# MLP weight tiles placed at rotating byte offsets, and the second layer's input moved by 224 bytes

## The chip, the cores and the metric

The kernel runs on one core of one Trainium2 chip. The metric is device time in microseconds (us) for one execution of the whole program; smaller is better. The core's engines run side by side and meet at semaphores: TensorE (PE, matmuls; its weight loads are shown as PEld), VectorE (DVE), ScalarE (ACT), GpSimd (POOL) and SyncE (SP, which issues the DMAs). Operands of a matmul lie in SBUF, 128 partitions with one address space in each; its result goes to PSUM.

## The reference

```python
x = A_u                                          # (1, 2048, 448)
mod = (silu(c) @ w_mod).reshape(c.shape[0], 6, 1, -1)
sa, ca, ga, sb, cb, gb = (mod[:, k] for k in range(6))
h = layernorm(x) * (1 + ca) + sa
x = x + ga * S4D(h)                              # a convolution over the 2048 tokens, by FFT in the reference
h = layernorm(x) * (1 + cb) + sb
# token-mixing MLP
h = layernorm(h)                                 # (1, 2048, 448)
u = gelu(einsum("bsd,sf->bdf", h, w1) + b1)      # w1: 2048 x 1792
y = einsum("bdf,fs->bds", u, w2) + b2            # w2: 1792 x 2048
x = x + gb * y.transpose(0, 2, 1)
```

All arrays are float32. The part that matters here is the MLP at the end: two products with weight matrices of 2048 x 1792 and 1792 x 2048, each against 448 channels.

## The kernel before

The first 57% of the program computes the modulation, the S4D convolution (with transforms written as matmuls) and the sum with `x`. The MLP follows, and there TensorE has hardly a gap.

**The MLP's split.** Each product is made with three matmuls in `float32r`, a form of float32 that TensorE takes in one pass. A weight tile `w` (128 partitions x 896 elements) is split into a high part `whi` (ScalarE, line 207) and a low part `wlo` = `w` - `whi` (VectorE, line 216). The other side is split in the same way: the normed input into `h3h` and `h3l`, the gelu's output into `uh` and `ul`. Then come high x high, high x low and low x high: lines 1373 to 1375 in the first layer (the function `mlp1`), lines 1442 to 1444 in the second. The weights are the stationary operand, 128 x 128 at a time (the weight load, PEld); the other side streams past them, 128 x 448 (the moving operand). That makes 672 matmuls in each layer, 1344 in all.

**The weight stream.** `WeightStream` numbers 64 weight tiles, n = 0 to 31 for the first layer and 32 to 63 for the second. `load` issues the DMA of a tile into one of 3 buffers of `w`; `begin` makes the high part, `rest` the low part and the next load. `whi` and `wlo` have `WAHEAD` = 4 buffers each, so the split runs up to four tiles ahead of the matmuls and then waits for a buffer.

**Where things lie.** The pools hand out SBUF addresses; the weight pool `mw` stands at the right end of SBUF, and the pools `mx` (the sums `xt`) and `mr` (layer norm's scratch) lie to its left. The pools `mk` (`h3h`, `h3l`) and `mu` (`uh`, `ul`) are filled from the left. A slice of 128 weight columns is 512 bytes, a row of a moving operand 1792 bytes, which is 7 x 256, a buffer of `whi` or `wlo` 3584 bytes, which is 14 x 256. So the address modulo 256 of a tile is that of all its slices and of all its buffers. In the program before, every slice of `whi` and `wlo` begins at 224 modulo 256, and every row of `h3h`, `h3l`, `uh` and `ul` at 32. For brevity this number is called the operand's place below.

The order of the work in the MLP is written out by hand on TensorE, ScalarE, VectorE and GpSimd (`manual_schedule`).

Of the kernel before, what the change touches and what calls it, by code (L numbers as in the profile page):

```python
# [11 lines left out]
F32 = mybir.dt.float32  # L12
F32R = mybir.dt.float32r
# [9 lines left out]
P = 128  # L23
# [13 lines left out]
WAHEAD = 4  # L37
# [117 lines left out]
def token_rows(a):  # L155

    return a.rearrange("(n g h r) d -> r g n h d", g=2, h=2, r=16)
# [8 lines left out]
class WeightStream:  # L166
# [4 lines left out]
    def __init__(self, tc, ctx, i):  # L171
        self.nc = tc.nc
        self.pool = ctx.enter_context(tc.tile_pool(name="mw", bufs=WAHEAD, side="right", reuse_waits="tile"))
        self.w1 = token_rows(i["B_w1"])
        self.w2 = i["B_w2"].rearrange("(k p) s -> p k s", p=P)
        self.raw, self.parts = {}, {}
        self.loaded = self.done = 0

# [20 lines left out]
    def begin(self, most):  # L199

        n = self.done
        if n >= min(most, 64):
            return None
        w = self.raw.pop(n)
        hi = self.pool.tile([P, 896], F32R, tag="whi", name="whi")
        lo = self.pool.tile([P, 896], F32R, tag="wlo", name="wlo")
        self.nc.scalar.copy(hi, w)  # L207
        self.parts[n] = hi, lo
        self.done += 1
        return w, hi, lo  # L210
# [11 lines left out]
def tile_adaln_s4d_mixer(ctx, tc, i, out):  # L222
# [21 lines left out]
    with ExitStack() as es:  # L244
# [827 lines left out]
        for s in range(tail):  # L1072
# [89 lines left out]
            if s == 16:  # L1162
                spec.close()
                up = early.enter_context(tc.tile_pool(name="up", bufs=3, reuse_waits="tile"))
# [190 lines left out]
    with ExitStack() as es:  # L1355
# [3 lines left out]
        up = es.enter_context(tc.tile_pool(name="mu", bufs=1))  # L1359
        pacc = es.enter_context(tc.tile_pool(name="pacc", bufs=7, space=PSUM))  # L1360
        h3h = kp.tile([P, 16, D], F32R, name="h3h")
        h3l = kp.tile([P, 16, D], F32R, name="h3l")
        uh = [up.tile([P, 7, D], F32R, name="uh0"), None]
        ul = [up.tile([P, 7, D], F32R, name="ul0"), None]

# [65 lines left out]
        for t in range(16):  # L1431
# [4 lines left out]
            for kh in range(2):  # L1436
                n = 32 + 2 * t + kh
                wst.ahead(n + WAHEAD, V)
                hi, lo = wst.parts.pop(n)
# [36 lines left out]
```

## Time and profile before

| | us |
|---|---|
| median of 3 runs | 690.65 (687.97 to 694.99) |
| the profiled execution | 685.43 |
| its span, first to last instruction | 683.7 |
| matmuls of the MLP, first to last start | 393.7 to 678.6 |
| TensorE busy in all | 612.7 (90%) |

The profiled execution took 1.7 us more than its span, and 5.2 us less than the median of the runs. A row that describes a group of instructions reads: line, engine, operation, out<-in by the program's names, shapes, count, then busy time in us and mean ns of one, then idle time before them with what ended it. A matmul's duration is from its start to its last result; the next one starts before that, so what a matmul costs in a stream is the distance from its start to the start of the next. PEclk is the granted share of TensorE's clock.

### The profile page before, as it was taken

What the parts mean: (1) busy time and instruction counts of PE and PEld (TensorE: products, weight loads), DVE (VectorE), ACT (ScalarE), POOL (GpSimd) and SP (SyncE); (2) the same over time, 40 slices, a digit from 0 to 9 for tenths busy, and PEclk for the clock granted to TensorE, in tenths of its full rate; (3) what the DMA queues carried; (4) which work ended last, traced back from release to release, by engine and by line L of the source; (5) the groups of instructions that cost most, each with busy time, mean ns of one, the idle gap of its engine ahead of it and who ended that gap; (6) DMA issues with size and microseconds to landing.
All of it is one profiled execution on the core that took longest, in us unless ns stands there. A gap on an engine that the chain in (4) does not pass through costs nothing. (4 is left out here: it accounts for less than half of the span.)

```text
span 683.7 us, 18263 instructions
## 1 busy us (share of the span) xinstructions
PE 612.7 (90%) x7180; PEld 456.0 (67%) x7180; DVE 452.6 (66%) x870; ACT 439.0 (64%) x880; POOL 268.1 (39%) x323
## 2 busy tenths in 40 slices
PE   0786778879989899989989899999999999999997
PEld 0443345535535556565657677779999999999996
DVE  7498799888779596895967587777422454433331
ACT  5967597988988999999945588877322322222220
POOL 6397457448458889789847100000000000000000
PEclk9989888999999999999999999999999999999999
DMA  7695563377896857344359799956674355555530
GB/s 176 199 201 111 181 200 120 128 269 223 251 310 190 234 116 216 97 133 136 97 140 315 237 256 255 239 128 199 160 221 135 95 142 168 165 161 170 167 119 28
DMA packets 105923, 121.14 MB, mean 177 GB/s; under 512 B 13098, under 2 KB 94286, under 8 KB 105710
## 3 DMA queue, kind: packets, MB, share of 16 engines
q1 hardware_dynamic: 104478, 113.92, 58.1%
q0 software_dynamic: 1360, 6.06, 4.1%
q8 instruction: 57, 0.93, 0.6%
q14 instruction: 28, 0.23, 0.1%
HBM read 84.59 MB, written 34.87 MB: 175 GB/s over the span
## 5 line engine op out<-in xcount | busy, mean ns | idle before, releaser
L207 ACT CAST whi<-w 128x896 fp32r<-128x896 f32 x64 | 59.8, 940 | 132.2 <-PE o L1443 84.5
L679 POOL TENSOR_TENSOR G<-mag,gs 128x512 f32<-128x512 f32 x56 | 71.8, 1281 | 66.1 <-ACT gs L675 65.9
L216 DVE TENSOR_TENSOR wlo<-w,whi 128x896 fp32r<-128x896 f32 x64 | 68.0, 1086 | 40.3 <-ACT whi L207 27.9
L1373 PE MATMUL acc<-h3h,whi 128*128 128x448 f32 x224 | 83.3, 372 | 1.6 <-ACT h3h L1278 1.6
L1374 PE MATMUL acc<-h3l,whi 128*128 128x448 f32 x224 | 82.1, 367 | 0.1
L1443 PE MATMUL o<-ul,whi 128*128 128x448 f32 x224 | 81.3, 363 | 0.0
L1375 PE MATMUL acc<-h3h,wlo 128*128 128x448 f32 x224 | 81.2, 362 | 0.0
L1442 PE MATMUL o<-uh,whi 128*128 128x448 f32 x224 | 81.2, 362 | 0.0
L1444 PE MATMUL o<-uh,wlo 128*128 128x448 f32 x224 | 80.6, 360 | 0.0
L710 PEld LDWEIGHTS kg<-E,G 128*32 128x32 f32 x3584 | 57.3, 116 | 34.9 <-issue 14.5
L627 PE MATMUL xg<-tab,lph 64*128 64x512 f32 x112 | 62.9, 563 | 12.4 <-DVE E L687 4.7
L710 PE MATMUL kg<-E,G 128*32 128x64 f32 x3584 | 67.1, 230 | 7.0 <-issue 3.3
L680 POOL TENSOR_TENSOR G<-mag,gs 128x512 f32<-128x512 f32 x56 | 71.8, 1282 | 0.0
L627 PE MATMUL xe<-tab,lph 64*128 64x512 f32 x112 | 63.5, 569 | 4.7 <-ACT gs L676 2.6
L1446 DVE SCALAR_TENSOR_TENSOR y<-o,b,mod 128x448 f32<-128x448 f32 x16 | 10.9, 684 | 80.2 <-PE o L1444 80.2
L656 POOL TENSOR_TENSOR m<-mag,w 128x512 f32<-128x512 f32 x56 | 58.9, 1052 | 4.4
L681 DVE TENSOR_TENSOR E<-m,xe 128x512 f32<-128x512 f32 x56 | 38.1, 681 | 23.2 <-ACT xe L674 19.8
L1373 PEld LDWEIGHTS acc<-h3h,whi 128*128 128x128 f32 x224 | 42.4, 189 | 14.6 <-ACT h L1283 5.6
L627 PE MATMUL xe<-tab,lex 64*128 64x512 f32 x56 | 30.9, 569 | 19.2 <-DMA lex<-wm 17.0
L1375 PEld LDWEIGHTS acc<-h3h,wlo 128*128 128x128 f32 x224 | 42.3, 189 | 3.0
L1442 PEld LDWEIGHTS o<-uh,whi 128*128 128x128 f32 x224 | 42.0, 188 | 3.4
L1374 PEld LDWEIGHTS acc<-h3l,whi 128*128 128x128 f32 x224 | 42.4, 190 | 2.7 <-DVE h3l L1281 0.5
(239 smaller groups left out, 1440.1 us busy)
## 6 DMA issues: line engine op xcount, KB each, us to landing
w<-in_B_w_dram SPq DMA_DIRECT2D x64, 224.0 KB
w<-in_B_w_dram SPq DMA_DIRECT2D x32, 448.0 KB
yu_d<-yt SPq DMA_DIRECT2D x16, 448.0 KB
yi<-yu_d SPq DMA_DIRECT2D x16, 448.0 KB
us_d<-uo SPq DMA_DIRECT2D x16, 448.0 KB
u<-us_d SPq DMA_DIRECT2D x32, 224.0 KB
v_d<-vt SPq DMA_DIRECT2D x32, 224.0 KB
vt<-v_d SPq DMA_DIRECT2D x14, 448.0 KB
```

The lines of the kernel that those rows point to most:

```text
L207: self.nc.scalar.copy(hi, w)
L216: eng.tensor_tensor(lo, w, hi.bitcast(F32), ALU.subtract)
L627: T.matmul(out[k], lhs[r], rhs[r], start=start, stop=stop)
L679: G.tensor_tensor(Gt[:, 1], mg_, v32(sg), ALU.mult)
L680: G.tensor_tensor(Gt[:, 0], mg_, v32(cg_), ALU.mult)
L710: T.matmul(kgs[g][32 * q : 32 * q + 32, m], Gt[:, c, d], E[:, c, d], start=h == 0 and c == 0 and m == 0, stop=h == 1 and c == 1, skip_grou ...
L1373: nc.tensor.matmul(acc[f], hi[:, fs], h3h[:, r], start=r == 0, stop=False)
L1374: nc.tensor.matmul(acc[f], hi[:, fs], h3l[:, r], start=False, stop=False)
L1375: nc.tensor.matmul(acc[f], lo[:, fs], h3h[:, r], start=False, stop=r == 15)
L1442: nc.tensor.matmul(o, hi[:, ks], uh[kh][:, k], start=kh == 0 and k == 0, stop=False)
L1443: nc.tensor.matmul(o, hi[:, ks], ul[kh][:, k], start=False, stop=False)
L1444: nc.tensor.matmul(o, lo[:, ks], uh[kh][:, k], start=False, stop=kh == 1 and k == 6)
```

## The change

Three tags of the weight pool are now asked for ahead of the others, so that they get their addresses in this order: `w` (3 x 3584 bytes), `whi` (4 buffers, now 920 elements = 3680 bytes), and a `gap` of 128 bytes; `wlo` (4 x 3680 bytes) follows. A buffer of 3680 bytes is 14 x 256 + 96, so each buffer's start is 96 further modulo 256 than the one before. Four of them and the gap make 58 x 256: a buffer of `wlo` has the same place as the buffer of `whi` of the same number. Within its buffer, the tile n begins at 8 x (n // 4 % 4) elements, so 0, 32, 64 or 96 bytes, for four tiles each. The pool `mu` gets 56 more elements, 224 bytes, ahead of `uh` and `ul`.

```diff
         self.w2 = i["B_w2"].rearrange("(k p) s -> p k s", p=P)
+        for t, m, b in (("w", 896, 3), ("whi", 920, WAHEAD), ("gap", 32, 1)):
+            self.pool.tile([P, m], F32R if t == "whi" else F32, tag=t, name=t, bufs=b)
         self.raw, self.parts = {}, {}
...
         w = self.raw.pop(n)
-        hi = self.pool.tile([P, 896], F32R, tag="whi", name="whi")
-        lo = self.pool.tile([P, 896], F32R, tag="wlo", name="wlo")
+        at = 8 * (n // 4 % 4)
+        hi, lo = (self.pool.tile([P, 920], F32R, tag=t, name=t)[:, at : at + 896] for t in ("whi", "wlo"))
         self.nc.scalar.copy(hi, w)
...
         h3l = kp.tile([P, 16, D], F32R, name="h3l")
+        up.tile([P, 56], F32, name="gap0")
         uh = [up.tile([P, 7, D], F32R, name="uh0"), None]
```

The addresses of the two built programs, modulo 256 (the buffers are taken in the order 0, 3, 2, 1):

| | before | after |
|---|---|---|
| `whi`, `wlo`, tiles n = 0 to 3 | 224 | 96, 128, 32, 192 |
| n = 4 to 7 | 224 | 128, 160, 64, 224 |
| n = 8 to 11 | 224 | 160, 192, 96, 0 |
| n = 12 to 15, and so on every 16 tiles | 224 | 192, 224, 128, 32 |
| `h3h`, `h3l` (moving, first layer) | 32 | 32 |
| `uh`, `ul` (moving, second layer) | 32 | 0 |
| `w` (landing of the weight DMAs) | 224 | 96 |

The pools `mx` and `mr` lie 896 bytes lower than before. The instructions of each engine, their order, the semaphores they wait for and their shapes are the same in both programs, row for row; only addresses differ.

## The prediction

> **What bounds the kernel now.** I read the page first: its chain of waits, then the groups of instructions, and then TensorE's stretch in the second layer.
>
> ```profile
> span 683.7 us, 18263 instructions
> PE 42%; ACT 1%; DVE 1%; issue 0%; ACTq 0%
> L1373 PE MATMUL acc<-h3h,whi 128*128 128x448 f32 x224 | 83.3, 372 | 1.6 <-ACT h3h L1278 1.6
> L1443 PE MATMUL o<-ul,whi 128*128 128x448 f32 x224 | 81.3, 363 | 0.0
> L1442 PE MATMUL o<-uh,whi 128*128 128x448 f32 x224 | 81.2, 362 | 0.0
> L1444 PE MATMUL o<-uh,wlo 128*128 128x448 f32 x224 | 80.6, 360 | 0.0
> ```
>
> The chain ends in TensorE for 42% of the span, and its lines are the MLP's matmuls. The right-hand column is the idle time in front of them: 0.0 in the second layer. Next, the stretch of that layer by busy time, and the tile `uh` with the first and last start of line 1442.
>
> ```profile
> core 0: us, PE busy (x) PEld busy (x) DVE busy (x) ACT busy (x) POOL busy (x), PEclk, DMA share, GB/s
> 544.00:678.50 134.50, 134.50 (x674) 126.06 (x674) 54.09 (x70) 29.85 (x33) 0.00 (x0) 1.00 0.50 141
> L1442 PE MATMUL o<-uh,whi x224: 362/362/363, 544.4 to 678.2; 128*128 128x448 f32 x112
> ```
>
> TensorE is busy for all of the 134.5 us, at a granted clock of 1.00, while VectorE is busy for 54 us and ScalarE for 30. Line 1442 comes once in three matmuls: 678.2 - 544.4 = 133.8 us over 223 steps is 600 ns for three, so 200 ns for one. The timeline of TensorE and of its weight loads shows the step itself (start in us, duration in us):
>
> ```profile
> 560.02 0.36 PE L1442 MATMUL o<-uh,whi 128*128 128x448 f32 x1
> 560.23 0.36 PE L1443 MATMUL o<-ul,whi 128*128 128x448 f32 x1
> 560.43 0.36 PE L1444 MATMUL o<-uh,wlo 128*128 128x448 f32 x1
> 560.62 0.36 PE L1442 MATMUL o<-uh,whi 128*128 128x448 f32 x1
> ...
> 560.03 0.19 PEld L1443 LDWEIGHTS o<-ul,whi 128*128 128x128 f32 x1
> 560.23 0.19 PEld L1444 LDWEIGHTS o<-uh,wlo 128*128 128x128 f32 x1
> ```
>
> A load of the next weights begins with each matmul and takes 0.19 of its 0.20 us. So the MLP's end is set by 1344 steps of 200 ns, 1344 x 0.2 = 268.8 us, and by nothing that the splitting of weights does. The waits say the same: ScalarE waits for TensorE to give a buffer of `whi` back, for 84.5 + 38.5 us, while TensorE's loads wait for ScalarE's split for 1.4 us.
>
> ```profile
> ACT whi L207 <- PE o L1443: 84.5, 27, 3.3
> ACT whi L207 <- PE acc L1374: 38.5, 13, 3.3
> ACT whi L207 <- DMA w<-in_B_w_dram: 9.0, 4, 4.4
> PEld acc L1373 <- ACT whi L207: 1.4, 2, 0.7
> ```
>
> **The change part by part.** No instruction, wait or shape changes, so only a duration or a step can.
>
> The landing place of the weight DMAs, the split's writes on ScalarE and VectorE, and the pools `mx` and `mr` that slide by 896 bytes: cost nothing. What hides them is the 84.5 + 38.5 us for which the split waits for TensorE. If that cover were gone, the 9.0 us of ScalarE's waits for `w` are what could come through; I take none of it. Layer norm's matmul (line 1243) reads `vt` from another place, but it is an ordinary float32 matmul, of the kind of which the next paragraph shows that it doesn't mind.
>
> The matmul's step is the one term that matters: 1344 x (its new length - 200 ns). The trace of before has every MLP matmul with weights at place 224 and the moving rows at 32, so it doesn't show the dependence; it must be bounded. First, how much of the 200 ns could be a stall at all? At the start of the MLP the clock is still halved (second row: granted clock 0.50), and the steps there are 395.63 - 395.26 = 0.37 us:
>
> ```profile
> 395.26 0.57 PE L1373 MATMUL acc<-h3h,whi 128*128 128x448 f32 x1
> 395.63 0.57 PE L1374 MATMUL acc<-h3l,whi 128*128 128x448 f32 x1
> ...
> 395.20:396.80 1.60, 1.60 (x6) 1.38 (x6) 1.47 (x6) 1.34 (x4) 0.00 (x0) 0.50 1.04 291
> ```
>
> At the full clock that would be 0.37 / 2 = 0.185 us, so up to 15 ns of the 200 are something that doesn't scale with the clock. The other float32 matmuls in the trace give a second value. Line 1253 streams 224 columns, in two passes (16 calls in the code, x32 in the row):
>
> ```profile
> 380.29 1.49 PE L1253 MATMUL y<-vt,fl 128*128 128x224 f32 x7
> ...
> L1253 PEld LDWEIGHTS y<-vt,fl x32: 186/190/190, 380.0 to 389.0; 128*128 128x128 f32 x32
> L1253 PE MATMUL y<-vt,fl x32: 352/352/457, 380.0 to 389.2; 128*128 128x224 f32 x32
> ```
>
> Seven of them in 1.49 us, the last one 0.352 long, make a step of (1.49 - 0.352) / 6 = 190 ns, again with a whole load of 128 x 128 weights beside each (190 ns). Its duration is 352 ns, where the MLP's are 362, 363 and 360: 10, 11 and 8 ns more, 29 in three. That is my price for the stall of a one-pass matmul with weights loading: 29 / 3 = 9.7 ns, 448 x 29 = 13.0 us in the MLP. In line 1253 `vt` lies at places 32 and 160 with `fl` at 32, and the median and the minimum are both 352: at that slower rate place does not matter.
>
> The Trainium skill ("TensorE: Matmul & The Clock Gate", Back-to-back issue gap) gives an isolated warm step as columns / 2.4 + 2.5 ns, 189 for 448 columns. The trace does not agree, with 200; by the page's step the MLP would have 1344 x 11 = 15 us to win, by line 1253's row 13.0.
>
> Is the stall one of place? The only other one-pass matmuls are in line 627 (one form of TensorE's work in the first half), where weights and moving operands all lie at 32:
>
> ```profile
> L627 PE MATMUL xe<-ones,mg x112: 376/386/647, 25.6 to 339.1; 64*128 64x512 bf16 x112
> L627 PE MATMUL xe<-tab,lex x56: 387/498/1305, 17.0 to 313.9; 64*128 64x512 f32 x56
> ```
>
> Minimum and median of the bfloat16 form are 376 and 386, the least of the float32r form is 387 (its median has waits in it). So a stall of 10 or 11 ns appears here too, with the two operands at the same place instead of 192 apart, another type and 512 columns instead of 448. One size at two distances looks like a fixed cost of the step and not like a meeting of two addresses. That is why my value for the term is 0. Its bounds: -13.0 us, if every stall goes; upwards no row has a larger stall that is surely one, and I take as much again, +13.0 us, since a conflict at one distance may well be twice as long at another.
>
> The sum: 685.43 + 0 = 685.43 us for the profiled execution. The runs' median is 5.2 us above it, at 690.65, so I forecast 690 us.
>
> **The rivals.** *Faster: the stall is a meeting of the two reads at distance 192, and rare elsewhere.* Both TensorE streams read SBUF, and the tiles after the change stand at all eight multiples of 32, at distance 192 in only 2 of 16 tiles in the first layer and 3 of 16 in the second. For it: the steps of 0.21, 0.20 and 0.19 us in the timeline add up to the 600 ns that hold on average over 223 of them, so the stall is systematic; and at the half clock it is gone. Against it: line 627's same stall at distance 0. If all but the tiles at 192 lose it, 13.0 x (1 - 5/32) = 11.0 us: 679.7 us; if half of the tiles lose it, 684.2. The page's rule of 189 ns is the end of this case. Speaking against this case is the skill's same page (What happens when you issue a matmul), by which moving operand and weight loads have independent read ports; line 1253's full load at no cost agrees, the 10 ns of the MLP leave it open.
>
> *Slower: the same mechanism, but 192 is one of the better distances.* Then the rotation leads most tiles to places with more stall. Priced by line 627: 387 may not be typical at distance 0; if a meeting costs the MLP as much again on every tile, +13.0 us, 703.7; on half of them 697.2. It decides against the kernel from a mean step of 205 ns on (5.2 x 1344 = 7 us). TensorE has no idle time here, so all of it reaches the end. For it: nothing but that the distance now is one of eight and not known to be bad.
>
> *No net change, though place matters:* some tiles at 190 and others at 210 ns, whose sum stays within 7 us. This gives my number too, 684 to 697.
>
> *The change does nothing it says:* the addresses of the built program are as in the table, so this has no chance of its own.
>
> **How the numbers follow.** A measurement of this kernel can tell about 1% (7 us) from no change; its three runs spread over 7.0 us. No effect of place: 0.42. Place matters, but the mean stays within 7 us: 0.13, together 0.55 for 'the same', between 684 and 697. Faster by over 1%: 0.26; it lies between 677.6 (all 13.0 us) and 684. Slower by over 1%: 0.19, between 697 and 704. The range runs from 677 to 701: it takes in the whole faster case, since -13.0 us rests on two rows, and the nearer half of the slower one. The likeliest case's own range is 684 to 697.
>
> **What would show it.** In the profile after: lines 1373 to 1375 and 1442 to 1444 still at 362, 363 and 360 ns on every tile, 600 ns for three, and the second layer 134 us long. If the durations of the MLP's matmuls differ from tile to tile, in a cycle of 16 tiles, then place matters, and the forecast is right only by its sum; durations near 352 would be the faster rival, 370 and more the slower. Line 1253 should keep its 352 ns. If ScalarE stops waiting for TensorE at line 207, or TensorE's idle time rises above 0.0 at line 1442, then the split has become the bound, which I have priced at nothing.

## The result, and the profile after

The changed kernel takes 693.80 us in the median of 18 runs (690.08 to 697.17), the kernel before 689.04 us in the median of 18 on the same chips (685.08 to 695.20). The ratio is 1.0064 with a 95% interval of 1.0044 to 1.0085: slower by about two thirds of a per cent. That is inside the forecast's range and within its 1%, but it is not the "no effect" that stood behind the number. All times below that are called "one execution" come from a single profiled run.

The page after has the same chain and the same groups as before (line, engine, operation, out<-in, shapes, count, then busy time and mean ns of one, then idle time before it). The line numbers are three higher.

```profile
span 691.1 us, 18263 instructions
PE 42%; ACT 1%; DVE 1%; issue 0%; ACTq 0%
L1376 PE MATMUL acc<-h3h,whi 128*128 128x448 f32 x224 | 83.7, 374 | 1.4 <-ACT h3h L1280 1.4
L1447 PE MATMUL o<-uh,wlo 128*128 128x448 f32 x224 | 81.8, 365 | 0.0
L1445 PE MATMUL o<-uh,whi 128*128 128x448 f32 x224 | 81.8, 365 | 0.0
L1446 PE MATMUL o<-ul,whi 128*128 128x448 f32 x224 | 81.6, 365 | 0.0
```

The second layer's matmuls last 365 ns on average where they lasted 360 to 363, and nothing waits in front of them. The busy time by stretch, cut at the first start of each layer and at the end, shows how much that is. Before, then after:

```profile
393.70:544.40 150.70, 150.65 (x724) 128.78 (x725) 88.24 (x216) 86.97 (x165) 0.00 (x0) 0.99 0.74 190
544.40:678.50 134.10, 134.10 (x672) 125.69 (x672) 53.73 (x69) 29.45 (x33) 0.00 (x0) 1.00 0.50 141
```

```profile
core 0: us, PE busy (x) PEld busy (x) DVE busy (x) ACT busy (x) POOL busy (x), PEclk, DMA share, GB/s
397.10:549.90 152.80, 152.56 (x724) 128.70 (x725) 88.31 (x216) 86.80 (x165) 0.00 (x0) 0.99 0.69 188
549.90:686.40 136.50, 136.50 (x674) 125.95 (x672) 53.65 (x69) 29.37 (x33) 0.00 (x0) 1.00 0.47 139
```

From start to start, at full resolution, the first layer went from 150.73 to 152.80 us and the second from 134.20 to 136.19: +2.07 and +1.99, together 4.06 us of the 4.76 us between the medians. TensorE is busy through both layers, the clock and the other engines are as they were. The MLP also begins 3.5 us later in this execution; across the kernels of this document, whose first part is the same, it begins anywhere between 393.7 and 401.3 us, so that is not put down to the change.

In streams of 448 columns at the full clock a matmul's duration stands 161 to 163 ns above its step in the traces here (362 at steps of 200), so durations can be read as steps. Line 1445 in the whole layer, and then in three single tiles of seven matmuls each (count, durations min/median/max in ns, first and last start):

```profile
L1445 PE MATMUL o<-uh,whi x224: 358/365/373, 549.9 to 685.7; 128*128 128x448 f32 x112
...
L1445 PE MATMUL o<-uh,whi x7: 358/367/372, 554.2 to 557.8; 128*128 128x448 f32 x7
L1445 PE MATMUL o<-uh,whi x7: 369/369/369, 579.8 to 583.5; 128*128 128x448 f32 x7
L1445 PE MATMUL o<-uh,whi x7: 362/362/363, 592.6 to 596.2; 128*128 128x448 f32 x7
```

Before, every tile had 362. Now one tile has 369 throughout, another 362, a third swings between 358 and 372. Taking each tile's mean step from the starts (without its first step), and the distance of its weights' place from its moving rows' place (modulo 256, places as in the table of addresses), gives an order that is the same in both layers, although the moving rows stand at 32 in the first and at 0 in the second:

| distance, bytes | tiles of 63 | mean step of a tile, ns |
|---|---|---|
| 0 | 6 | 202.4, 202.5; one 206.4 |
| 32 | 6 | 203.3, 204.3 |
| 64 | 5 | 201.9 to 202.4 |
| 96 | 10 | 200.0 to 201.1; one 206.7 |
| 128 | 10 | 203.6 to 204.1 |
| 160 | 10 | 205.2 to 205.4 |
| 192 | 10 | 199.9 to 200.3 |
| 224 | 6 | 206.6, 206.7; 204.5; one 200.0 |

(The first tile is left out: part of it runs at half clock. Gaps where layer norm's matmuls stand between are left out too.) The mean over the 63 tiles is 202.90 ns, before it was 200.05; 1344 x 2.85 = 3.8 us, nearly all of the 4.06. The distance before, 192, is the lowest row of the table, and no tile falls below it. Within a tile the steps repeat in a short cycle, for instance 201, 198, 201 ns at distance 192 and 203, 212, 200, 209, 196 at 128; such a cycle is called a rhythm below.

The parts that were costed at nothing did cost nothing: ScalarE still waits for TensorE to hand `whi` back (86.6 + 39.7 us), and the two-pass float32 matmuls of layer norm keep their 352 ns with `vt` in another place.

```profile
ACT whi L209 <- PE o L1446: 86.6, 27, 3.4
ACT whi L209 <- PE acc L1377: 39.7, 13, 3.4
...
L1255 PE MATMUL y<-vt,fl x32: 352/352/457, 383.5 to 393.0; 128*128 128x224 f32 x32
```

### The profile page after: what moved, and what is told of

It reads as the page before. It is cut to its first block, busy times and chain, and to the rows that moved or that the text cites. A ratio compares the mean times of both kernels' runs of the same rounds, so it can differ in the third digit from the quotient of the medians.

```text
span 691.1 us, 18263 instructions
## 1 busy us (share of the span) xinstructions
PE 621.6 (90%) x7180; PEld 458.0 (66%) x7180; DVE 452.5 (65%) x870; ACT 438.9 (64%) x880; POOL 268.6 (39%) x323
## 5 line engine op out<-in xcount | busy, mean ns | idle before, releaser
L209 ACT CAST whi<-w 128x896 fp32r<-128x896 f32 x64 | 59.7, 938 | 134.7 <-PE o L1446 86.6
L640 ACT ACTIVATE mag<-xe 128x512 f32<-128x512 f32 x56 | 35.7, 637 | 13.9 <-PE xe L629 6.2
```

## The experiments

**1. One part alone: the 224 bytes ahead of the second layer's input.** The weights stay at 224, so the first layer keeps distance 192 and the second gets 224.

```diff
+        up.tile([P, 56], F32, name="gap0")
         uh = [up.tile([P, 7, D], F32R, name="uh0"), None]
```

> Only the second layer's input is moved, by 224 bytes; the weights stay at place 224. Distance of weights to moving rows, modulo 256: 192 in the first layer as before, 224 in the second. Theory A (the distance of the two reads sets the step): first layer unchanged at 600 ns for three matmuls, durations 362, 363, 360; second layer as the tiles at distance 224 in the changed kernel, 613 to 620 ns for three, so 3 to 4.5 us longer than before. Rival B (the place of the weights alone, or of the input alone, sets the step): with the weights at 224 the second layer stays at 600 ns for three if it is the weights; if it is the input's place 0, it takes the changed kernel's 136.2 us.

Measured: 693.1 us, ratio 1.0061 (1.0026 to 1.0095). Windows of the two layers, and line 1443 with its durations:

```profile
395.40:546.10 150.70, 150.68 (x725) 128.85 (x726) 88.45 (x216) 86.75 (x165) 0.00 (x0) 0.99 0.73 190
546.10:684.90 138.80, 138.80 (x673) 126.14 (x671) 53.65 (x69) 29.51 (x33) 0.00 (x0) 1.00 0.47 136
...
L1443 PE MATMUL o<-uh,whi x224: 369/369/369, 546.1 to 684.3; 128*128 128x448 f32 x112
```

The first layer is untouched, the second takes 138.67 us from start to start, 4.5 more (672 x 6.7 ns = 4.5). So one number in the allocation, with no instruction changed, moves the mean step of a whole layer. Place matters, and a bad place costs more than the rotation's mixture.

**2. Finer places.** The tiles begin 4, 8, 12, 16, 20 bytes and so on into their buffers, so that distances in steps of 16 and 4 bytes occur.

```diff
-        at = 8 * (n // 4 % 4)
+        at = (4, 12, 20, 1, 12, 4, 1, 20, 4, 12, 20, 1, 2, 3, 5, 7)[n // 4]
```

> The changed kernel with its tiles at other offsets, so that the distance takes all multiples of 16 and, in some tiles, multiples of 4 bytes. Theory A (a load of weights and the moving rows meet modulo 256 about twice in every load, wherever they start): no distance is much below 200 ns a step, and distances between two multiples of 32 lie between or near their neighbours. Rival C (only whole steps of 32 bytes are bad, some finer distance escapes): some tiles come down to 189 or 190 ns, durations near 352.

Measured in one execution: 691.4 us, tile means between 200.0 and 206.7 ns, 152.4 and 136.5 us for the layers from start to start. Distances 36, 108, 200 and 212 stand at 200.0 or 200.1, distances 16, 44, 116, 132 and 148 at 206.6 or 206.7. Neighbours 4 bytes apart differ (112 gives 204, 116 gives 206.7, 108 gives 200.0), so there is no "safe" multiple. Most of these distances stand in one tile only, and experiment 9 shows that what went before a tile counts as well. Still, no tile is below 200.

**3. High and low parts interleaved**, so that the weights are read with a stride of 8 bytes and meet the moving row at other moments.

```diff
-        hi = self.pool.tile([P, 896], F32R, tag="whi", name="whi")
-        lo = self.pool.tile([P, 896], F32R, tag="wlo", name="wlo")
+        at = 4 * (n // 4 % 2)
+        whl = self.pool.tile([P, 904, 2], F32R, tag="whl", name="whl")
+        hi, lo = (whl[:, at : at + 896, c] for c in range(2))
```

> High and low parts of a weight tile are interleaved, element by element, so that a load of 128 columns takes every second element and walks through 1024 bytes in the time in which it walked through 512; the distance at the start of a load rotates through all multiples of 32 within 8 tiles. Theory A (the moving rows advance twice as fast as the load, catch up with it modulo 256, and each meeting costs about 5 ns): at twice the pace the load runs alongside the moving rows and keeps its distance, so most tiles take 189 to 192 ns a step, and those that start at the bad distance take well over 207. Rival D (the 10 ns are a fixed cost of a one-pass step, and place only adds to it): 200 to 207 ns on all tiles, as in the changed kernel; more on all of them if a load with a stride is slower.

Measured in one execution: 691.5 us, tiles between 200.0 and 205.5 ns. The loads (first row) became 7 ns longer, which shows that the stride took effect:

```profile
L1443 PEld LDWEIGHTS o<-uh,whl x224: 193/195/199, 548.0 to 683.8; 128*128 128x128 f32 x112
L1443 PE MATMUL o<-uh,whl x224: 361/366/374, 548.2 to 684.0; 128*128 128x448 f32 x112
```

A stall that came from load and moving row stepping through the same places side by side should have gone on most tiles. It did not; that theory fell here.

**4. Half the load.** 64 weight columns instead of 128 in all but the first and last matmul of each sum; the other half of the result is left out.

```diff
...
-                    nc.tensor.matmul(o, hi[:, ks], uh[kh][:, k], start=kh == 0 and k == 0, stop=False)
...
+                    m = P if 7 * kh + k in (0, 13) else 64
+                    ks = slice(k * P, k * P + m)
+                    nc.tensor.matmul(o[0:m], hi[:, ks], uh[kh][:, k], start=kh == 0 and k == 0, stop=False)
...
```

> The kernel before, with weight slices of 64 columns instead of 128 except in the first and last step of each sum: half of each result is left out. Everything else, the moving rows of 448 columns above all, is as before. Theory A (meetings of the two reads, as many as the load is long): one meeting instead of two, so about half of the stall: steps of 194 to 195 ns, durations near 357, the MLP 6 us shorter. Rival D (a fixed cost of a one-pass step): 200 ns, durations 360 to 363.

Measured in one execution: 689.4 us.

```profile
L1446 PEld LDWEIGHTS o<-uh,whi x224: 133/134/188, 547.1 to 681.9; 128*64 128x64 f32 x96, 128*128 128x128 f32 x16
L1446 PE MATMUL o<-uh,whi x224: 360/362/371, 547.3 to 682.1; 128*64 128x448 f32 x96, 128*128 128x448 f32 x16
```

The load fell from 188 to 134 ns, and the second layer's step is 201.4 ns on average, no shorter than before. The stall does not shrink with the load.

**5. All tiles at distance 224** (both moving operands 224 bytes higher, weights as before).

```diff
+        kp.tile([P, 56], F32, name="gap0")
         h3h = kp.tile([P, 16, D], F32R, name="h3h")
```

> The kernel before with the moving operands of both layers 224 bytes higher (place 0), the weights fixed at 224: distance 224 in all 1344 matmuls. Theory A2 (the distance sets the step, at 224 it is 206.7 ns as in the second layer of the run with only the input moved): 1344 x 6.7 = 9.0 us more than before in the MLP, ratio 1.013. Rival J (the long step of that run came from the change of distance between the layers, and a kernel with one distance settles at 200 ns): ratio 1.000.

Measured: 698.81 us in the median of six against 689.19, but five runs lay between 697.19 and 700.12 and one at 686.88, below the kernel before; an interval would mean nothing for two groups, so none is given. In the profiled execution the second layer does not repeat the 369 ns of experiment 1:

```profile
L1443 PE MATMUL o<-uh,whi x224: 367/367/367, 556.0 to 692.8; 128*128 128x448 f32 x112
L1444 PE MATMUL o<-ul,whi x224: 363/363/363, 556.2 to 693.0; 128*128 128x448 f32 x112
L1445 PE MATMUL o<-uh,wlo x224: 367/367/368, 556.4 to 693.2; 128*128 128x448 f32 x112
```

Steps of 205, 202 and 206 in turn, 204.4 on average, from the second tile to the end of both layers. One distance has several stable rhythms: 206.7, 204.4, and 200.0 (one tile of the changed kernel). In this trace the first tile ends at 206.7 (steps of 207, 206 and 207); layer norm's matmuls come between it and the second tile, which runs at 204.4, and later interruptions of the same kind leave it there. So an interruption can change the rhythm and need not. The two layers together take 6.9 us more than in the trace before, less than the 9.6 us between the medians; this execution's MLP also begins at 401.3. The odd run of 686.88 would fit the rhythm of 200.0 held throughout, but it was not profiled: that the rhythm is what sets these runs apart is argued only.

**6. All tiles at distance 96**, the other low row of the table.

```diff
+        kp.tile([P, 24], F32, name="gap0")
         h3h = kp.tile([P, 16, D], F32R, name="h3h")
```

> As the run with all matmuls at distance 224, with the moving operands at place 128: distance 96 everywhere. In the changed kernel tiles at distance 96 took 200 ns, and one of them (n = 20) 207. If the distance alone sets the step: 200 ns everywhere, the MLP as long as before. If the distance allows two rhythms and the entry chooses: stretches at 200 and stretches at 206.7 ns, the MLP 0 to 9 us longer.

Measured in one execution: 689.1 us; from start to start the layers take 150.87 and 134.20 us, as before.

```profile
396.90:547.60 150.70, 149.34 (x724) 127.64 (x725) 88.07 (x216) 86.79 (x165) 0.00 (x0) 1.00 0.71 191
547.60:682.10 134.50, 134.50 (x674) 126.07 (x672) 53.79 (x69) 29.68 (x33) 0.00 (x0) 1.00 0.49 141
```

So the moving rows can stand at another place without loss, and 200 ns is not special to distance 192: distance 96 holds it through both layers, and no float32r tile of any run is clearly below it.

**7. Very short loads, and in the first layer shorter rows** (16 weight columns; 256 moving columns in the first layer, 448 in the second; most of the result is left out). The diff is that of experiment 4 with 16 for 64, and in the first layer `h3h[:, r, 0:c]` with c = 256.

> The kernel before with weight slices of 16 columns, except in the first and last step of each sum; in the first layer only 256 of 448 columns move. Most of the result is left out. Theory D (the 10 to 13 ns are a fixed cost of each one-pass step, whether a load runs beside it or not): first layer 256/448 x 186.7 + 13.3 = 120 ns a step, second layer 200 to 202 ns. Rival F (the rows are supplied a little slower than they stream, so the stall grows with the columns): first layer 256/448 x 200 = 114 ns, second layer 200 ns. Rival A (the load beside the stream stalls it): second layer near 190 ns, the load being an eighth as long.

Measured in one execution, 659.0 us:

```profile
L1375 PEld LDWEIGHTS acc<-h3h,whi x224: 92/94/329, 396.1 to 513.4; 128*16 128x16 f32 x98, 128*128 128x128 f32 x14
L1375 PE MATMUL acc<-h3h,whi x224: 275/278/575, 396.1 to 513.6; 128*16 128x256 f32 x98, 128*128 128x448 f32 x14
...
L1446 PEld LDWEIGHTS o<-uh,whi x224: 94/95/189, 514.0 to 651.5; 128*16 128x16 f32 x96, 128*128 128x128 f32 x16
L1446 PE MATMUL o<-uh,whi x224: 360/369/370, 514.2 to 651.7; 128*16 128x448 f32 x96, 128*128 128x448 f32 x16
```

With a load of 95 instead of 188 ns, the second layer's step at distance 192 is 206.7 ns through most of each tile: half the load, and the worst rhythm at the best distance. So the distance doesn't decide the rhythm alone, and a stall that grows while the load is halved is not time that the load takes. In the first layer eleven tiles have 116.7 ns per step throughout, about as many settle at 113.3, and three have 120.0: three rhythms at one distance. 256/448 of 200 is 114, of 206.7 is 118, and of the 189.2 ns that a step takes without a stall (experiment 8) it is 108. So the stall there is some 5, 9 or 12 ns in place of 11 to 17: it tends to shrink with the row, as something that accrues per column would. The tiles at 120 ns, near what a fixed stall of 11 ns would give, keep this from being a clean proof.

A second sign that no load is needed was in the trace before. At the end of each of the first twelve tiles of the first layer the next weights load only 0.29 to 0.30 us after the last matmul's start (one such end; matmuls first, then the loads):

```profile
405.84 0.36 PE L1374 MATMUL acc<-h3l,whi 128*128 128x448 f32 x1
406.05 0.37 PE L1375 MATMUL acc<-h3h,wlo 128*128 128x448 f32 x1
406.34 0.60 PE L1243 MATMUL y<-vt,ft 128*64 128x448 f32 x2
...
405.85 0.19 PEld L1375 LDWEIGHTS acc<-h3h,wlo 128*128 128x128 f32 x1
406.34 0.20 PEld L1243 LDWEIGHTS y<-vt,ft 128*64 128x64 f32 x4 [0.31 <-DVE h3l L1285]
```

The matmul at 406.05 has no load beside it until 0.29 us after its start and lasts 0.37 us, not the 0.352 of a matmul without a stall. At the eleven other such ends it is 0.36 us, as in line 1375's matmuls with a load beside them, and still more than 0.352.

**8. Two bytes per column.** The same high and low parts are read as their upper 16 bits (the lower bits are left out). In the first layer the operands stay where they are and every second 16-bit element is read, so a column still advances by 4 bytes; in the second layer `uh` and `ul` are written as packed 16-bit rows.

```diff
-                nc.tensor.matmul(acc[f], hi[:, fs], h3h[:, r], start=r == 0, stop=False)
...
+                h = lambda t: t.bitcast(BF16)
+                w = lambda t: h(t)[:, 2 * f * P + 1 : 2 * (f + 1) * P : 2]
+                x = lambda t: h(t[:, r])[:, 1 : 2 * D : 2]
+                nc.tensor.matmul(acc[f], w(hi), x(h3h), start=r == 0, stop=False)
...
-        uh[1] = up.tile([P, 7, D], F32R, name="uh1")
+        uh[1] = up.tile([P, 7, D], BF16, name="uh1")
```

> The kernel before with bfloat16 operands in the MLP, which leaves out the low mantissa bits: in the first layer every second 2-byte element of the float32 tiles is read (4 bytes of SBUF walked per column, as before), in the second layer the moving rows are packed bfloat16 (2 bytes per column). Theory H (the stall comes from moving 4 bytes per column at the full clock): second layer near 189 ns a step, durations near 352; the first layer at 200 ns if the bytes that are walked count, at 189 if the bytes that are delivered count. Theory D (fixed cost of each one-pass step): 200 ns in both.

Measured in one execution: 677.8 us.

```profile
L1376 PEld LDWEIGHTS <-whi x224: 96/97/144, 393.7 to 543.2; 128*128 128x128 bf16 x112
L1376 PE MATMUL acc<-h3h,whi x224: 358/358/575, 395.7 to 543.4; 128*128 128x448 bf16 x112
...
L1446 PEld LDWEIGHTS <-whi x224: 97/98/98, 543.8 to 670.4; 128*128 128x128 bf16 x112
L1446 PE MATMUL o<-uh,whi x224: 351/352/353, 544.0 to 670.6; 128*128 128x448 bf16 x112
```

This pair tells the two suspects apart. Both layers have the same type and the same short load (97 and 98 ns), and both read their weights with a stride. Where the moving row advances 4 bytes per column, the step is 197.8 ns; where it advances 2, it is 189.2 and the duration 352, in every tile. The load is the same, so the 8.6 ns between them belong to the moving row. They are most of the 10.8 ns that float32r loses at the same distance; whether its remaining 2 ns come from the type was not separated.

**9. The rotation alone**, without the 224 bytes (the change less `gap0`).

> The rotation of the weights alone, without the 224 bytes ahead of the second layer's input: both layers' moving rows start 32 bytes into a multiple of 256, so both layers see the same eight distances of weights and moving rows. Theory (the distance chooses the rhythm): layer 1 as in the changed kernel, 152.8 us, and layer 2 136.2 us within 0.5 as well, since the same eight distances come up in it; 693 us. Rival (the places of the moving rows count by themselves, as the 224 bytes alone cost layer 2 4.5 us): layer 2 stays nearer to the kernel before, 134.2 to 135 us, and the whole is at 691 to 692 us.

Measured in one execution: 152.82 and 136.35 us for the layers from start to start, the tiles in the main as in the table by distance. The whole is 697.6 us because the MLP began at 401.3 in this execution. Both layers now lose about 2 us, so the rotation is enough for the whole loss; the 224 bytes add nothing to it. The run also shows how a rhythm depends on what went before. The same tile position (distance 224, the weights in the same buffer at the same offset), in the first layer and in the second:

```profile
L1375 PE MATMUL acc<-h3h,whi x7: 362/362/475, 463.5 to 467.2; 128*128 128x448 f32 x7
...
L1444 PE MATMUL o<-uh,whi x7: 369/369/369, 601.1 to 604.8; 128*128 128x448 f32 x7
```

In the first layer four of layer norm's matmuls (line 1245) stand directly ahead of this tile; in the second the MLP's own matmuls run into it without a break.

**10. A version without the stall.** All parts, of weights and inputs, are made and stored as packed 16-bit numbers (ScalarE and VectorE write them so); no rotation, no gap. The product keeps some 16 bits of each factor.

```diff
-        hi = self.pool.tile([P, 896], F32R, tag="whi", name="whi")
-        lo = self.pool.tile([P, 896], F32R, tag="wlo", name="wlo")
+        hi = self.pool.tile([P, 896], BF16, tag="whi", name="whi")
+        lo = self.pool.tile([P, 896], BF16, tag="wlo", name="wlo")
...
-        h3h = kp.tile([P, 16, D], F32R, name="h3h")
-        h3l = kp.tile([P, 16, D], F32R, name="h3l")
+        h3h = kp.tile([P, 16, D], BF16, name="h3h")
+        h3l = kp.tile([P, 16, D], BF16, name="h3l")
```

> Both layers' high and low parts, of weights and inputs, are made and stored as packed 16-bit numbers (the product keeps some 16 bits of each factor instead of nearly all of them), everything else as before, no rotation and no gap. Theory (the stall goes with four bytes of moving row per column at the full clock): 189 ns per step in both layers, so layer 1 (150.7 us before, 150.1 us of it in 672 steps at about 200 ns and the sixteen or so at half clock) falls by 672 x 11 ns = 7.4 us to about 143, layer 2 by the same to 127; the whole 675 us, ratio 0.979. Rival 1 (16-bit operands load in another way, with loads that end later or issue apart): steps of 198 ns as in layer 1 with every second 16-bit element, 688 us. Rival 2 (layer 1 becomes bound by the copies that make the parts, or by the weights' transfers, once its steps are shorter): layer 1 stays above 147 us with idle time ahead of a tile's first matmul, 678 to 682 us.

Measured: 673.14 us in the median of six, ratio to before 0.9769 (0.9732 to 0.9805). It beats both kernels, by 15.8 us the one before.

```profile
L1373 PE MATMUL acc<-h3h,whi 128*128 128x448 bf16 x224 | 79.9, 357 | 1.7 <-ACT h3h L1278 1.7
L1442 PE MATMUL o<-uh,whi 128*128 128x448 bf16 x224 | 78.9, 352 | 0.0
...
L1442 PEld LDWEIGHTS <-whi x224: 97/98/98, 543.2 to 669.8; 128*128 128x128 bf16 x112
L1442 PE MATMUL o<-uh,whi x224: 352/352/353, 543.4 to 669.9; 128*128 128x448 bf16 x112
...
ACT whi L207 <- PE o L1443: 77.8, 27, 3.0
ACT whi L207 <- PE acc L1374: 32.2, 11, 3.0
```

Layers of 143.7 and 126.9 us from start to start instead of 150.7 and 134.2: the step is 189.2 ns in all tiles but those at the clock's change and one with a wait. TensorE stays the bound, since ScalarE still waits for it for 110 us.

**11. The same with the change on top**: 16-bit weights rotating by 0, 32, 64 and 96 bytes, high and low parts at one place, the second layer's input 224 bytes higher.

> As the 16-bit kernel beside it, but with the change on top: the 16-bit weights rotate by 0, 32, 64 and 96 bytes, high and low parts one place modulo 256, and the second layer's input 224 bytes higher. Theory (a packed 16-bit moving row is supplied faster than it streams, so there is no rhythm to lock into): 189 ns at every distance, the same time as the 16-bit kernel without the rotation within 1.5 us, 675 us. Rival (the clash of weights and moving rows is there at 16 bits too, and the 189 ns of layer 2 at 16 bits was a good distance): some tiles at 194 to 200 ns, and 3 to 8 us more than the kernel without the rotation.

Measured: 673.37 us, ratio 0.9762 (0.972 to 0.9804), no difference from experiment 10.

```profile
L1445 PE MATMUL o<-uh,whi x224: 352/352/353, 536.9 to 663.4; 128*128 128x448 bf16 x112
L1447 PE MATMUL o<-uh,wlo x224: 352/352/353, 537.3 to 663.8; 128*128 128x448 bf16 x112
```

With 2 bytes per column every place is alike: the very change that costs 4 us in float32r costs nothing here.

**12. The changed kernel once more**, unaltered, for a second trace.

> The changed kernel once more, unaltered, for one more trace. Theory (each distance has a few rhythms, and which one a tile falls into is settled as it begins, differently from run to run): most tiles have the same mean step as in the first trace within 0.5 ns, some have another of the values 200.0, 202.2, 203.3, 204.4, 205 and 206.7, layers 152.3 to 153.3 and 135.7 to 136.7 us, 693 us. Rival (the rhythm follows from the distance and what went before alone): all 64 half-tiles repeat within 0.2 ns.

Measured: 692.0 us; the layers take 152.83 and 136.19 us from start to start, where the first trace has 152.80 and 136.19. All tiles from the third on repeat their mean step within 0.1 ns. So my own expectation, that the rhythm differs from run to run, was wrong for this kernel, as far as two traces show: the rhythm follows from the distances and from what went before. The first two tiles differ by 0.6 ns between the traces, and the third agrees again. Whether a kernel with one distance everywhere keeps what it happened to begin with, as the runs of experiment 5 suggest, no second trace shows.

## Why the prediction was right or wrong

**What bounds the kernel:** right. TensorE's 1344 steps set the time of the MLP, with no idle time before or after the change, and everything the matmul step lost reached the end (4.06 us in the MLP, 4.76 between the medians).

**Everything but the step at nothing:** right. The split's waits, the pools that slide and line 1253 (now 1255) are unchanged.

**The size of the stall:** right in the main, 13.0 us forecast against 14.6. The price was 29 ns in three steps, 13.0 us in the MLP, from the 352 ns of line 1253. Experiment 10 takes the whole stall away and arrives at exactly that duration, at 189.2 ns per step: (200.05 - 189.2) x 1344 = 14.6 us. The Trainium skill ("TensorE: Matmul & The Clock Gate", Back-to-back issue gap) has columns / 2.4 + 2.5 ns for an isolated step, which makes an estimate of 448 / 2.4 + 2.5 = 189.2 ns. The packed 16-bit kernel agrees with it to the digit; the float32r kernels, at 200 to 207, do not.

**The term that failed: "1344 x (its new length - 200 ns)", valued at 0** because line 627's stall of 10 or 11 ns at equal places "looks like a fixed cost of the step and not like a meeting of two addresses". It measured +2.85 ns per step, 3.8 us. The stall is neither of the two things that I set against each other. It is not fixed, since it takes 11 to 17 ns by distance; and it is not a meeting of two reads that goes away elsewhere, since at none of the 39 distances of the table and of experiment 2 is a tile's mean step clearly below 200. Two rows at two distances were too few to conclude from: by the table, distance 0 (202.5) and distance 192 (200.0) are 2.5 ns apart, so a look at just these two could only say "equal". And line 627 was no measure of this stall. Its matmuls start two at a time, and the 376 and 386 ns are both durations of packed 16-bit rows (`ones`), which lose nothing in the MLP of experiments 10 and 11. The float32r form's least, 387, is no longer than these rows' median, so the row doesn't tell a stalled step from a free one:

```profile
145.53 0.39 PE L627 MATMUL xe<-ones,mg 64*128 64x512 bf16 x1
145.53 0.39 PE L627 MATMUL xg<-ones,mg 64*128 64x512 bf16 x1
...
145.75 0.38 PE L627 MATMUL xe<-ones,mg 64*128 64x512 bf16 x1
```

**The rivals:** the faster one is refuted in its outcome by the table: 192 is not a bad distance, and no other is free of the stall. Experiments 3, 4 and 7 speak against its mechanism, since neither the stride nor the length of the load takes the stall away. That the weights' place sets the size of the stall shows that the two reads do bear on each other, in a way that stays open. The slower one had the mechanism in its heading, "192 is one of the better distances", and this is what the table shows; it had too high a price (as much stall again, 6.5 to 13 us), and the mean of 202.9 stayed under the 205 ns from which it was to decide. The third, some tiles at 190 and others at 210 with a sum within 7 us, is the case that came, except that nothing stands at 190.

**The test named in the prediction** held: durations that differ from tile to tile in a cycle of 16 tiles mean that place matters and the forecast is right only by its sum. That is the state of things: 690 forecast, 693.8 measured, and the reason for the number was wrong. That it came so close is luck: this mixture of distances averages 2.85 ns, where the worst rhythm throughout would have cost 1344 x 6.7 = 9 us.

**What stays open:** why a distance gives its rhythm. The steps of a tile repeat in short cycles (201, 198, 201 at distance 192; 200, 209, 196, 204, 211 at 128) whose means are close to 200.0, 202.4, 203.3, 204.4, 205 and 206.7, which looks as if the stall came in lumps that lock to something periodic; no run shows what. Neither the load's length nor its stride predicted which. It was not tried whether 4-byte weights under a packed 2-byte moving row would stall.

## What to carry to other kernels

When steps of a back-to-back matmul stream are longer than the same engine's best step elsewhere in the trace, ask what the moving row must be fed, per column, before asking where it lies: here 4 bytes per column of float32r cost 11 to 17 ns on 448 columns at every distance tried, and 2 packed bytes cost none. A change of addresses can move such a stream by up to 3% of a step without one instruction changing, so compare the distance of its two operands, modulo 256, before and after any change of allocation, and keep it if it is at the floor. Read the step itself from the trace as well, since one distance can hold several rhythms. And a dependence on place is not excluded by two points that agree.

## What the runs showed of the hardware

- A one-pass float32r matmul of 448 columns at the full clock takes 200.0 to 206.7 ns per step by the distance of weights and moving rows; packed 16-bit takes 189.2 at all eight distances, and 16-bit elements read at a stride of 4 bytes take 197.8 (one distance, 192).
- The distance counts more than either place: the order of the table is the same with rows at 32 and at 0. With weights at 224 throughout, rows at 32 (before), 0 (experiment 1, second layer) and 128 (experiment 6) give 200.0, 206.7 and 200.0.
- One distance can hold more than one rhythm (224: 200.0, 204.4 and 206.7 ns; 192 with short loads: 206.7 where full loads have 200.0). The six runs of the kernel with 224 throughout spread over 13 us (686.88 to 700.12), against 10 us for 18 runs of the kernel before; one of them was profiled.
- A load of 128 x 128 weights takes 188 ns in float32r and 98 in 16 bits, and 95 with only 16 columns of float32r. With a load of 95 ns the second layer's step at distance 192 rose from 200.0 to 206.7 through most of each tile.
